# Square root and reciprocal for the first LayerNorm rows, and a new order of the first loads, turns and matmuls

## The chip, the cores and the metric

The kernel runs on one core of one Trainium2 chip. The metric is the device time of one execution in microseconds (us); less is better. The core has TensorE (matrix products, PE in the profile, with PEld for the loading of its stationary operand), VectorE (DVE), ScalarE (ACT), GpSimd (POOL) and SyncE (SP, which here only issues DMAs). 16 DMA engines move data between HBM and SBUF. PSUM has 8 buffers of 128 x 512 float32 in this kernel.

## The reference

```python
xn = layernorm(x)                       # x: 2048 rows of 512, eps 1e-5
dt, Lam = exp(log_dt), Lambda_re + 1j * Lambda_im
Lam_bar = exp(dt * Lam)
B_bar = ((Lam_bar - 1) / Lam)[:, None] * (B_re + 1j * B_im)
Bu = xn @ B_bar.T                       # 2048 x 512, complex
h[t] = Lam_bar * h[t - 1] + Bu[t]       # over 2048 steps
A = 2 * (h @ (C_re + 1j * C_im).T).real + xn * Dskip
B = (silu(xn @ w1) * (xn @ w3)) @ w2    # w1, w3: 512 x 1792, w2: 1792 x 512
out = x + A + B
```

Inputs and output are bfloat16.

## The kernel before

The 2048 rows are four blocks of 512, and a block is four groups of 128 rows. For a block the kernel normalises the rows, turns them so that the 512 columns lie on the partitions (`xnT`), multiplies by w1 and w3 in 14 tiles of 128 columns (`glu_up`, lines 372 to 397: `g_ps` and `u_ps`, then Silu and a copy on ScalarE, their product on VectorE), by the state matrices (`ssm_in`, line 402), runs the recurrence as a scan on VectorE (`ssm_tasks`, line 419), and adds the products with w2 and C into one sum (`y_out`, line 475). VectorE's work is a queue of tasks with written costs, from which `drain` takes some after each matmul tile, so the order of every engine's instructions is fixed by the program text (manual schedule); an engine runs its own in that order.

The change concerns the start, block 0 (lines 79 to 147 and 499 to 547). There:

- The loads. SP issues rows 0 to 127 and 128 to 255 (`load_rows`, lines 79 and 80), then w1 and w3 in pieces (`load_w13`, lines 111 to 116). ScalarE issues `load_prm` of Lambda_re, then rows 256 to 511 in one load, then Lambda_im and log_dt (lines 107 to 110). The three parameter vectors land in 12 rows of `prm`.
- For each group c: `stats(c)` and `aggr(c)` (VectorE: mean and variance), `rstd_act` (ScalarE, lines 167 to 170: `Ln` with the bias tensor `eps`, then `Exp` with scale -0.5; both from one table set, loaded at line 81), `normed` (VectorE, line 186), `turn` (TensorE transposes into PSUM, line 247) and `put` (a copy to `xnT`, line 251: ScalarE for groups 0 and 1, VectorE for 2 and 3).
- `keep_warm` (line 145) puts matmuls of ones on TensorE: 8 of 512 columns and 5 of 128 at the start, and 3 of 128 between the turns of groups 0 and 1.
- `ahead(w_sbs, fs, c, n)` (line 499) multiplies the rows of groups c to c+n-1 for the tiles fs of the first three glu tiles, whose PSUM buffers (`begun`) are held from the start. What is left of these tiles, rows 384 to 511, is done in `glu_up` (lines 376 to 383).
- The parameters: a TensorE transpose of `prm` (line 539) into PSUM, and `par_cols` (line 267): a ScalarE copy, an Exp for dt, small products on GpSimd. A further Exp (line 545) makes `r_col`. Then the table set with Silu is loaded (line 546).

PSUM: six buffers for the three begun tiles and two (`xt_a`, `xt_b`) for the turns. Tiles 3 and later take buffers as they come free.

The text of the start, in order (lines 508 to 547), is in the listing's end.

Of the kernel before, what the change touches and what calls it, by code (L numbers as in the profile page):

```python
# [12 lines left out]
ACT = mybir.ActivationFunctionType  # L13

FP32 = DT.float32
BF16 = DT.bfloat16
P = 128
# [3 lines left out]
def kernel(  # L21
# [24 lines left out]
    nc = tc.nc  # L46
# [9 lines left out]
    NPT = PS // P  # L56
    NFT = F // P
    assert S % TBLK == 0 and D % P == 0 and F % P == 0 and PS == NPT * P and D == 512 and NPT == 4
    LN_EPS = 1e-5
# [4 lines left out]
    const = ctx.enter_context(tc.tile_pool(name="const", bufs=1))  # L64
# [5 lines left out]
    def ps_tile(name):  # L70
        return psum.tile([P, 512], FP32, name=name, tag="ps")
# [4 lines left out]
    def load_rows(c0, c1, eng):  # L76
        eng.dma_start(out=x_blk[0][:, c0:c1, :], in_=xv[:, 0, c0:c1, :])

    load_rows(0, 1, nc.sync)
    load_rows(1, 2, nc.sync)  # L80
    nc.scalar.preload_act_table_set("natural_log_exp_and_others")
    w1_sb = const.tile([P, NDT, F], BF16, name="w1_sb")
    w3_sb = const.tile([P, NDT, F], BF16, name="w3_sb")
    w2_sb = const.tile([P, NFT, D], BF16, name="w2_sb")
# [16 lines left out]
    prm = const.tile([P, P], BF16, name="prm")  # L101
    nc.vector.memset(prm, 0.0)

    def load_prm(i, src, eng):
        eng.dma_start(out=prm[i * NPT:(i + 1) * NPT, :], in_=src.rearrange("(t p) -> t p", p=P))

    load_prm(0, A_Lambda_re, nc.scalar)
    load_rows(2, CPB, nc.scalar)
    load_prm(1, A_Lambda_im, nc.scalar)
    load_prm(2, A_log_dt, nc.scalar)  # L110
    load_w13(0, 2)
    load_w13(2, 4)
# [18 lines left out]
    eps = const.tile([P, 1], FP32, name="eps")  # L131
    nc.vector.memset(eps, LN_EPS)
    ident = const.tile([P, P], BF16, name="ident")
# [9 lines left out]
    begun = [(ps_tile("g_ps"), ps_tile("u_ps")) for _ in range(3)]  # L143

    def keep_warm(n, width=512):
        one = nc.const_aps.tensor_like(1.0, like=ident[:, 0:1])
        for _ in range(n):
            nc.tensor.matmul(out=begun[0][0][:, :width], lhsT=one.to_broadcast([P, P]), rhs=one.to_broadcast([P, width]),
                             start=True, stop=True)
# [5 lines left out]
    mv_all = const.tile([P, NBLK * CPB, 2], FP32, name="mv_all")  # L155
    rstd_all = const.tile([P, NBLK * CPB], FP32, name="rstd_all")
# [3 lines left out]
    def stats(c):  # L160
        sums[c] = work.tile([P, 6], FP32, name="stats", bufs=4)
        nc.vector.bn_stats(out=sums[c], in_=x_blk[c // CPB][:, c % CPB, :])  # L162

    def aggr(c):
        nc.vector.bn_aggr(out=mv_all[:, c, :], in_=sums.pop(c))  # L165

    def rstd_act(c0, c1):
        y = rstd_all[:, c0:c1]
        nc.scalar.activation(out=y, in_=mv_all[:, c0:c1, 1], func=ACT.Ln, bias=eps)  # L169
        nc.scalar.activation(out=y, in_=y, func=ACT.Exp, scale=-0.5)  # L170

    def rstd(c0, c1):
        y = rstd_all[:, c0:c1]
# [12 lines left out]
    def normed(c, parts=1):  # L186
        xn = work.tile([P, D], BF16, name="xn", bufs=8)
        for i in range(parts):
            ds = slice(i * D // parts, (i + 1) * D // parts)
            nc.vector.tensor_scalar(out=xn[:, ds], in0=x_blk[c // CPB][:, c % CPB, ds], scalar1=mv_all[:, c, 0:1],  # L190
                                    scalar2=rstd_all[:, c:c + 1], op0=ALU.subtract, op1=ALU.mult)
        return xn
# [51 lines left out]
    pprm = xt_a[:, NDT]  # L244
    xn0 = xns_of[0] = {}

    def turn(c, pxt, d0=0, d1=NDT):
        for dt in range(d0, d1):
            nc.tensor.transpose(out=pxt[:, dt - d0, :], in_=xn0[c][:, dt * P:(dt + 1) * P], identity=ident)  # L249

    def put(c, pxt, eng, d0=0, d1=NDT):
        dst = xnTs[0][:, d0:d1, c * P:(c + 1) * P]
        if eng is nc.scalar:
            nc.scalar.activation(out=dst, in_=pxt, func=ACT.Copy)
        else:
            nc.vector.tensor_copy(out=dst, in_=pxt)
# [3 lines left out]
    tabs = {k: const.tile([P, NPT, SB], BF16, name=f"tab_{k}") for k in ("x", "y", "c", "s")}  # L260
    col = {}

    def c4(name):
        col[name] = const.tile([P, NPT], FP32, name=f"c_{name}")
        return col[name]

    def par_cols():
        prmc = const.tile([P, 3 * NPT], FP32, name="prmc")
        nc.scalar.activation(out=prmc, in_=pprm[:, :3 * NPT], func=ACT.Copy)
        col["lre"], col["lim"], col["ldt"] = (prmc[:, i * NPT:(i + 1) * NPT] for i in range(3))  # L270
        nc.scalar.activation(out=c4("dt"), in_=col["ldt"], func=ACT.Exp)
        nc.gpsimd.tensor_tensor(out=c4("kr"), in0=col["dt"], in1=col["lre"], op=ALU.mult)
        nc.gpsimd.tensor_tensor(out=c4("ki"), in0=col["dt"], in1=col["lim"], op=ALU.mult)
        nc.gpsimd.tensor_scalar(out=c4("turn"), in0=col["ki"], scalar1=float(1.0 / (2.0 * np.pi)), scalar2=None,
                                op0=ALU.mult)
        tt = nc.gpsimd.tensor_tensor
        tt(out=c4("den"), in0=col["lre"], in1=col["lre"], op=ALU.mult)
        tt(out=c4("d2"), in0=col["lim"], in1=col["lim"], op=ALU.mult)
        tt(out=col["den"], in0=col["den"], in1=col["d2"], op=ALU.add)
# [73 lines left out]
    def drain(us):  # L353
        credit[0] = min(credit[0] + us, us + 1.5)
        while queue and credit[0] > 0:
            cost, task = queue.popleft()
            credit[0] -= cost
            task()
# [8 lines left out]
    def glu_mm(b, f, w_sb, ps, ts, dts=range(NDT)):  # L367
        for dt in dts:
            nc.tensor.matmul(out=ps[:, ts], lhsT=w_sb[:, dt, f * P:(f + 1) * P], rhs=xnTs[b][:, dt, ts],  # L369
                             start=(dt == 0), stop=(dt == NDT - 1))  # L370

    def glu_up(b, rate, begun=()):
        hg[b] = work.tile([P, NFT, TBLK], BF16, name="hgT")
        late = None
        for f in range(NFT):
            if f < len(begun):
                g_ps, u_ps = begun[f]
                ts = slice(TBLK - P, TBLK)
            else:
                g_ps, u_ps = ps_tile("g_ps"), ps_tile("u_ps")  # L380
                ts = slice(0, TBLK)
            glu_mm(b, f, w1_sb, g_ps, ts)
            glu_mm(b, f, w3_sb, u_ps, ts)
            sl16 = work.tile([P, TBLK], BF16, name="sl16", bufs=4)
            nc.scalar.activation(out=sl16, in_=g_ps, func=ACT.Silu)  # L385
            up16 = work.tile([P, TBLK], BF16, name="up16", bufs=4)
            nc.scalar.activation(out=up16, in_=u_ps, func=ACT.Copy)  # L387
            if for_act:
                for_act.popleft()()
            if late is not None:  # L390
                late()

            def late(f=f, sl16=sl16, up16=up16):
                nc.vector.tensor_tensor(out=hg[b][:, f, :], in0=sl16, in1=up16, op=ALU.mult)  # L394

            drain(rate)
        late()
# [101 lines left out]
    def ahead(w_sbs, fs, c, n=1, dts=range(NDT)):  # L499
        for f in fs:  # L500
            for w_sb in w_sbs:
                glu_mm(0, f, w_sb, begun[f][w_sb is w3_sb], slice(c * P, (c + n) * P), dts)
# [3 lines left out]
    ta, tb, t2, t3 = xt_a[:, :H], xt_b[:, :H], xt_b[:, NDT:], xt_a[:, :NDT]  # L506

    stats(0)
    aggr(0)
    rstd_act(0, 1)  # L510
    stats(1)
    aggr(1)
    rstd_act(1, 2)
    xn0[0] = normed(0, 2)
    turn(0, ta, 0, H)
    put(0, ta, nc.scalar, 0, H)
    xn0[1] = normed(1)
    turn(0, tb, H, NDT)
    put(0, tb, nc.scalar, H, NDT)
    keep_warm(3, P)  # L520
    turn(1, t1)
    put(1, t1[:, :H], nc.scalar, 0, H)
    put(1, t1[:, H:], nc.scalar, H, NDT)
    stats(2)
    aggr(2)
    rstd_act(2, 3)
    stats(3)
    ahead((w1_sb,), (0, 1), 0)
    ahead((w1_sb,), (0, 1), 1, 1, range(H))
    ahead((w1_sb,), (0, 1), 1, 1, range(H, NDT))  # L530
    xn0[2] = normed(2)
    aggr(3)
    rstd_act(3, 4)
    ahead((w3_sb,), (0, 1), 0, 2)
    turn(2, t2)
    put(2, t2, nc.vector)
    xn0[3] = normed(3)
    ahead((w1_sb,), (2,), 0, 2)
    nc.tensor.transpose(out=pprm, in_=prm, identity=ident)
    par_cols()  # L540
    ahead((w3_sb,), (2,), 0, 2)
    ahead((w1_sb, w3_sb), (0,), 2)
    turn(3, t3)
    put(3, t3, nc.vector)
    nc.scalar.activation(out=r_col, in_=col["kr"], func=ACT.Exp)
    nc.scalar.preload_act_table_set("silu_and_others")
    ahead((w1_sb, w3_sb), (1, 2), 2)

    push([(3.2, par_turns), (0.2, par_recip)])
    push([(0.0, lambda: for_act.extend(par_trig()))])  # L550
# [4 lines left out]
    push([(1.2, par_out)])  # L555
    push(ln_tasks(2))
    glu_up(0, 1.3, begun)
    assert not for_act
    ssm_in(0, 0.8)
# [3 lines left out]
    push(res_tasks(2))  # L563
    push(res_tasks(3))
    glu_up(1, 1.35)
    y_out(0, 4.0)
    ssm_in(2, 0.85)
    glu_up(2, 1.35)
    y_out(1, 4.0)
    ssm_in(3, 0.85)  # L570
# [33 lines left out]
```

## Time and profile before

| | us |
|---|---|
| median of 3 runs (lowest to highest) | 211.91 (211.91 to 212.12) |
| the profiled execution's own time | 211.86 |
| its span in the profile | 210.1 |
| TensorE busy | 205.4 |
| VectorE busy | 173.2 |
| ScalarE busy | 93.9 |
| GpSimd busy | 5.9 |
| granted TensorE clock | 0.998 |

The span is the time from the first to the last instruction of one execution on the chip, taken by the profiler. Times in the views below are us from its start. A row of the timeline has start, duration, engine, line, operation, what is written and read, the shape and the count; in square brackets stands how long the engine had been idle and what ended that. Neighbouring instructions of one line are merged into one row, so that a row's duration covers all of them. The duration of a matmul is modelled to the end of its pipeline; the distance from one start to the next is what TensorE spends on it.

Busy time by stage, from the view by windows (each engine's us and instruction count):

| window, us | PE | DVE | ACT |
|---|---|---|---|
| 0.00 to 4.88 | 4.01 (14) | 2.06 (9) | 2.04 (4) |
| 4.88 to 7.02 | 2.05 (27) | 1.98 (5) | 1.79 (8) |
| 7.02 to 11.95 | 4.93 (76) | 3.18 (10) | 3.40 (9) |
| 11.95 to 69.10 | 56.83 (262) | 53.83 (132) | 43.08 (76) |
| 69.10 to 210.10 | 137.55 (650) | 112.20 (193) | 43.62 (73) |

### The profile page before, as it was taken

The page shows a single profiled execution, that of the slowest core. Times are in us where ns is not written, and L with a number is a line of the kernel's source. Part 1 is how long each engine was busy: PE and PEld are TensorE (multiplying, and loading weights), DVE is VectorE, ACT ScalarE, POOL GpSimd, SP SyncE. Part 2 cuts the span into 40 slices and gives each one's busy share as a digit, 9 for nine tenths or more (in the row PEclk, how much of TensorE's full clock was granted, in tenths as well). Part 3 has the DMA queues.
Part 4 walks back from the last instruction along what each step waited for, and adds up shares of the span by engine and source line. Part 5 has one row for each costly group of instructions (what it writes and reads, how often), then busy time and mean ns, then how long its engine had stood idle before and what let it go on. Part 6 is the DMA issues. An engine that isn't in the chain of part 4 may idle for free.

```text
span 210.1 us, 2867 instructions
## 1 busy us (share of the span) xinstructions
PE 205.4 (98%) x1021; PEld 97.7 (47%) x1039; DVE 173.2 (82%) x345; ACT 93.9 (45%) x167; POOL 5.9 (3%) x27
## 2 busy tenths in 40 slices
PE   8999999999999999999999999999999999999994
PEld 3864444444444444444444444444444444444453
DVE  4699989979999999999999999999999999121111
ACT  4699867666666200066666500036666620000000
POOL 2100410000000000000000000000000000000000
PEclk9999999999999999999999999999999999999999
DMA  6999798965000000000004100100000000000110
GB/s 172 299 353 199 106 189 179 329 133 106 19 3 0 0 25 25 28 27 0 0 0 78 27 16 9 50 28 0 2 0 0 0 3 25 27 25 25 44 34 25
DMA packets 27094, 13.69 MB, mean 65 GB/s; under 512 B 15944, under 2 KB 27080, under 8 KB 27080
## 3 DMA queue, kind: packets, MB, share of 16 engines
q1 hardware_dynamic: 26784, 13.24, 26.8%
q10 hardware_dynamic: 296, 0.27, 0.4%
q8 instruction: 8, 0.13, 0.3%
q14 instruction: 6, 0.05, 0.1%
HBM read 7.74 MB, written 2.10 MB: 47 GB/s over the span
## 4 chain that ended last, share of the span: by engine, by line
PE 95%; DVE 1%; ACT 1%; DMA 1%; issue 1%; ACTq 0%
PE u_ps L369 23%; PE y_ps L485 23%; PE g_ps L369 22%; PE y_ps L490 13%; PE bu_ps L408 13%; DMA x_blk<-in_A_x_dram 1%; ACT up L387 1%; DVE stats L162 1%; PE xt_ps L249 0%; DVE xn L190 0%; PE g_ps L249 0%; DVE mv_all L165 0%; ACT rstd_all L169 0%; DVE o L495 0%; ACT rstd_all L170 0%
## 5 line engine op out<-in xcount | busy, mean ns | idle before, releaser
L369 PEld LDWEIGHTS <-w_sb 128*128 128x128 bf16 x504 | 46.6, 98 | 50.1
L369 PE MATMUL u_ps<-xnT,w_sb 128*128 128x512 bf16 (+2 forms) x247 | 58.3, 358 | 0.3
L369 PE MATMUL g_ps<-xnT,w_sb 128*128 128x512 bf16 (+2 forms) x249 | 57.6, 352 | 0.2
L485 PE MATMUL y_ps<-w_sb,hgT 128*128 128x512 bf16 (+2 forms) x233 | 50.7, 366 | 0.2
L387 ACT ACTIVATE up<-u_ps 128x512 bf16<-128x512 f32 x56 | 33.8, 603 | 15.2 <-PE u_ps L369 14.9
L410 ACT ACTIVATE u<-bu_ps 128x512 bf16<-128x512 f32 x32 | 19.1, 598 | 46.3 <-PE bu_ps L408 46.3
L385 ACT ACTIVATE sl<-g_ps 128x512 bf16<-128x512 f32 x56 | 33.7, 602 | 9.8 <-PE g_ps L369 8.2
L442 DVE TENSOR_TENSOR_SCAN ab<-r_col,h,ab 128x256 bf16<-128x256 f32 x56 | 37.7, 732 | 0.2
L485 PEld LDWEIGHTS <-hgT 128*128 128x128 bf16 x238 | 22.8, 98 | 25.9
L495 DVE TENSOR_TENSOR o<-y_ps,x_blk 128x512 bf16<-128x512 f32 (+2 forms) x17 | 11.1, 654 | 24.3 <-PE y_ps L490 24.3
L490 PE MATMUL y_ps<-ct,h 128*128 128x512 bf16 (+2 forms) x134 | 30.2, 366 | 0.1
L408 PE MATMUL bu_ps<-xnT,bt 128*128 128x512 bf16 x125 | 27.8, 379 | 0.2
L394 DVE TENSOR_TENSOR hgT<-sl,up 128x512 bf16<-128x512 bf16 x56 | 23.0, 414 | 2.2 <-ACT up L387 2.2
L490 PEld LDWEIGHTS <-h 128*128 128x128 bf16 x136 | 13.0, 98 | 14.7
L408 PEld LDWEIGHTS <-bt 128*128 128x128 bf16 x128 | 12.5, 98 | 15.1
L162 DVE BATCH_NORM_STATS2 stats<-x_blk 128x6 f32<-128x512 bf16 x16 | 10.6, 674 | 2.0 <-DMA x_blk<-in_A_x_dram 2.0
L451 DVE TENSOR_TENSOR ab<-ab,tab_s 128x2048 bf16<-128x2048 bf16 x8 | 9.8, 1224 | 0.2
L447 DVE TENSOR_TENSOR ab<-ab,tab_c 128x2048 bf16<-128x2048 bf16 x8 | 9.8, 1222 | 0.1
L427 DVE TENSOR_TENSOR ab<-u,tab_y 128x2048 bf16<-128x2048 bf16 x8 | 9.8, 1219 | 0.0
L424 DVE TENSOR_TENSOR ab<-u,tab_x 128x2048 bf16<-128x2048 bf16 x8 | 9.8, 1219 | 0.0
L199 DVE TENSOR_TENSOR x_blk<-xd,x_blk 128x512 bf16<-128x512 bf16 x16 | 6.8, 426 | 0.5
L198 DVE TENSOR_TENSOR xd<-xn,dskip_row 128x512 bf16<-128x512 bf16 x16 | 6.7, 418 | 0.0
(74 smaller groups left out, 80.1 us busy)
## 6 DMA issues: line engine op xcount, KB each, us to landing
w_sb<-in_B_w_dram SPq DMA_DIRECT2D x4, 512.0 KB, 7.7
out_dram<-o SPq DMA_DIRECT2D x15, 128.0 KB, 1.7
w_sb<-in_B_w_dram SPq DMA_DIRECT2D x1, 1792.0 KB, 9.1
w_sb<-in_B_w_dram SPq DMA_DIRECT2D x6, 256.0 KB, 4.8
x_blk<-in_A_x_dram SPq DMA_DIRECT2D x3, 512.0 KB, 5.9
x_blk<-in_A_x_dram SPq DMA_DIRECT2D x2, 128.0 KB, 2.1
x_blk<-in_A_x_dram ACTq DMA_DIRECT2D x1, 256.0 KB, 3.6
xnT<-xn SPq DMA_TRANSPOSE x12, 2.5
```

The costliest lines, as they stand in the source:

```text
L162: nc.vector.bn_stats(out=sums[c], in_=x_blk[c // CPB][:, c % CPB, :])
L369: nc.tensor.matmul(out=ps[:, ts], lhsT=w_sb[:, dt, f * P:(f + 1) * P], rhs=xnTs[b][:, dt, ts], start=(dt == 0), stop=(dt == NDT - 1))
L385: nc.scalar.activation(out=sl16, in_=g_ps, func=ACT.Silu)
L387: nc.scalar.activation(out=up16, in_=u_ps, func=ACT.Copy)
L394: nc.vector.tensor_tensor(out=hg[b][:, f, :], in0=sl16, in1=up16, op=ALU.mult)
L408: nc.tensor.matmul(out=u_ps, lhsT=bt[ri][:, dt, pt * P:(pt + 1) * P], rhs=xnTs[b][:, dt, :], start=(dt == 0), stop=(dt == NDT - 1))
L410: nc.scalar.activation(out=u16[:, :, pt, ri, :], in_=u_ps.rearrange("p (s t) -> p s t", s=NSB), func=ACT.Copy)
L424: nc.vector.tensor_tensor(out=ab[0][:, :, 0:2, :], in0=u16, in1=tab_b("x"), op=ALU.mult)
L442: nc.vector.tensor_tensor_scan(out=a[:, pt, 2 * ri + 1, :], data0=r_b, data1=a[:, pt, 2 * ri, :], initial=init, op0=ALU.mult, op1=ALU.add)
L485: nc.tensor.matmul(out=y_ps[:, ds], lhsT=hg[b][:, f, cl * P:(cl + 1) * P], rhs=w2_sb[:, f, ds], start=(f == 0), stop=False)
L490: nc.tensor.matmul(out=y_ps[:, ds], lhsT=h_tiles[i][:, pt, ri, h_ts], rhs=ct[ri][:, pt, ds], start=False, stop=(pt == NPT - 1 and ri == 1))
L495: nc.vector.tensor_tensor(out=o16[:, ds], in0=y_ps[:, ds], in1=x_blk[b][:, cl, ds], op=ALU.add)
```

## The change

ScalarE now makes the square root of variance plus 1e-5, with the constant in the instruction in place of the `eps` tensor, and VectorE makes its reciprocal (`rstd_inv`), which stands in VectorE's order where the diff puts it. The first table set is the one with Sqrt, and after group 3's Sqrt the set with Exp is loaded; Silu's set follows as before. On ScalarE's DMA queue, Lambda_im goes ahead of rows 256 to 511. The transpose of the parameters and ScalarE's copy of them become `par_turn`, ahead of group 3's aggregate. The turns of groups 2 and 3 stand together, behind all `ahead` pieces of rows 0 to 255 except tile 2 of w3, and tiles 1 and 2 take rows 256 to 511 in one piece of 256 columns, so that `glu_up` has matmuls of rows 384 to 511 for tile 0 alone. One of the three `keep_warm` matmuls goes.

```diff
-    nc.scalar.preload_act_table_set("natural_log_exp_and_others")
+    nc.scalar.preload_act_table_set("sqrt_and_others")
...
     load_prm(0, A_Lambda_re, nc.scalar)
+    load_prm(1, A_Lambda_im, nc.scalar)
     load_rows(2, CPB, nc.scalar)
-    load_prm(1, A_Lambda_im, nc.scalar)
     load_prm(2, A_log_dt, nc.scalar)
...
     def rstd_act(c0, c1):
         y = rstd_all[:, c0:c1]
-        nc.scalar.activation(out=y, in_=mv_all[:, c0:c1, 1], func=ACT.Ln, bias=eps)
-        nc.scalar.activation(out=y, in_=y, func=ACT.Exp, scale=-0.5)
+        nc.scalar.activation(out=y, in_=mv_all[:, c0:c1, 1], func=ACT.Sqrt, bias=LN_EPS)
+
+    def rstd_inv(c):
+        y = rstd_all[:, c:c + 1]
+        nc.vector.reciprocal(out=y, in_=y)
...
+    prmc = const.tile([P, 3 * NPT], FP32, name="prmc")
...
+    def par_turn():
+        nc.tensor.transpose(out=pprm, in_=prm, identity=ident)
+        nc.scalar.activation(out=prmc, in_=pprm[:, :3 * NPT], func=ACT.Copy)
+
     def par_cols():
-        prmc = const.tile([P, 3 * NPT], FP32, name="prmc")
-        nc.scalar.activation(out=prmc, in_=pprm[:, :3 * NPT], func=ACT.Copy)
...
-            glu_mm(b, f, w1_sb, g_ps, ts)
-            glu_mm(b, f, w3_sb, u_ps, ts)
+            if f == 0 or f >= len(begun):
+                glu_mm(b, f, w1_sb, g_ps, ts)
+                glu_mm(b, f, w3_sb, u_ps, ts)
...
     rstd_act(0, 1)
     stats(1)
+    rstd_inv(0)
     aggr(1)
     rstd_act(1, 2)
     xn0[0] = normed(0, 2)
     turn(0, ta, 0, H)
     put(0, ta, nc.scalar, 0, H)
+    rstd_inv(1)
     xn0[1] = normed(1)
     turn(0, tb, H, NDT)
     put(0, tb, nc.scalar, H, NDT)
-    keep_warm(3, P)
+    keep_warm(2, P)
     turn(1, t1)
...
     rstd_act(2, 3)
     stats(3)
+    rstd_inv(2)
     ahead((w1_sb,), (0, 1), 0)
     ahead((w1_sb,), (0, 1), 1, 1, range(H))
     ahead((w1_sb,), (0, 1), 1, 1, range(H, NDT))
-    xn0[2] = normed(2)
+    par_turn()
     aggr(3)
     rstd_act(3, 4)
+    nc.scalar.preload_act_table_set("exp_and_others")
+    xn0[2] = normed(2)
+    rstd_inv(3)
+    xn0[3] = normed(3)
     ahead((w3_sb,), (0, 1), 0, 2)
+    ahead((w1_sb,), (2,), 0, 2)
     turn(2, t2)
     put(2, t2, nc.vector)
-    xn0[3] = normed(3)
-    ahead((w1_sb,), (2,), 0, 2)
-    nc.tensor.transpose(out=pprm, in_=prm, identity=ident)
+    turn(3, t3)
+    put(3, t3, nc.vector)
     par_cols()
     ahead((w3_sb,), (2,), 0, 2)
     ahead((w1_sb, w3_sb), (0,), 2)
-    turn(3, t3)
-    put(3, t3, nc.vector)
     nc.scalar.activation(out=r_col, in_=col["kr"], func=ACT.Exp)
     nc.scalar.preload_act_table_set("silu_and_others")
-    ahead((w1_sb, w3_sb), (1, 2), 2)
+    ahead((w1_sb, w3_sb), (1, 2), 2, 2)
```

## The prediction

> **What bounds the kernel now.** I read the page's busy times first, then the chain that ended last, then the timeline of the first 13 us, instruction by instruction where merged rows hide starts.
>
> ```profile
> PE 205.4 (98%) x1021; PEld 97.7 (47%) x1039; DVE 173.2 (82%) x345; ACT 93.9 (45%) x167; POOL 5.9 (3%) x27
> ...
> PE 95%; DVE 1%; ACT 1%; DMA 1%; issue 1%; ACTq 0%
> ```
>
> TensorE is busy 98% of the span and makes 95% of the chain. Only a few us at the start belong to others. The change edits only those, so the question is when TensorE begins to run without a gap, and whether it gets a new one. In the timeline:
>
> ```profile
> 2.88 0.69 DVE L162 BATCH_NORM_STATS2 stats<-x_blk 128x6 f32<-128x512 bf16 x1 [1.95 <-DMA x_blk<-in_A_x_dram]
> ...
> 3.83 0.29 ACT L169 ACTIVATE rstd_all<-mv_all,eps 128x1 f32<-128x1 f32 x1 [1.83 <-DVE mv_all L165]
> 4.16 0.20 ACT L170 ACTIVATE rstd_all<-rstd_all 128x1 f32<-128x1 f32 x1
> 4.41 0.18 DVE L165 BATCH_NORM_AGGREGATE mv_all<-stats 128x2 f32<-128x6 f32 x1
> 4.50 1.10 DVE L190 TENSOR_SCALAR xn<-x_blk,mv_all,rstd_all 128x256 bf16<-128x256 bf16 x3
> 4.62 0.29 ACT L169 ACTIVATE rstd_all<-mv_all,eps 128x1 f32<-128x1 f32 x1 [0.27 <-DVE mv_all L165]
> ...
> 4.95 0.20 ACT L170 ACTIVATE rstd_all<-rstd_all 128x1 f32<-128x1 f32 x1
> ...
> 5.65 0.23 PEld L249 LDWEIGHTS <-xn 128*128 128x128 bf16 x4 [0.24 <-DVE xn L190]
> ...
> 6.09 0.66 ACT L254 ACTIVATE xnT<-g_ps 128x256 bf16<-128x256 bf16 x2 [0.23 <-PE g_ps L249]
> ...
> 7.02 1.04 PE L369 MATMUL u_ps<-xnT,w_sb 128*128 128x256 bf16 x8
> ```
>
> The reader is to see one chain: rows 0 land (2.86), VectorE's statistics, ScalarE's Ln and Exp for rows 128 to 255, VectorE's normalisation (5.185 to 5.601, the third of the x3), TensorE's turn (5.658), ScalarE's copies (6.092 to 6.750), TensorE's matmuls. From 7.022 on, every start to start distance is the matmul's own (0.056 us for 128 columns, 0.109 for 256, 0.216 for 512); a double one every 10.79 us is a missing record. So time moves only by what moves 7.022, by the sum of columns behind it, or by a new gap.
>
> **Sqrt and reciprocal for Ln and Exp.** No row shows Sqrt. Nearest: Exp without a bias tensor 0.202 us, a 12-column Copy 0.181, Ln with its bias tensor 0.295. I take 0.20, ends 0.18 and 0.295. RECIPROCAL on 128x4 took 0.172, other 128x4 VectorE operations 0.161 to 0.170. I take 0.17.
> Rows 0: Sqrt starts at 3.83 like Ln and ends at 4.03. The reciprocal stands behind the second statistics, whose 0.66 us free VectorE at about 4.285 for independent work, while the aggregate that needs their result starts at 4.406. In that hole of 0.12 us the reciprocal needs some 0.09 (14.04, and the next operation 14.13). Cost nothing; without the hole 0.09.
> Rows 128 to 255: Sqrt at 4.623 to 4.82 (4.92 at the upper end). But the reciprocal is queued on VectorE behind the two halves of the first normalisation, at 4.505 and 4.735. These free it after 0.23 to 0.26 us: 4.965 to 4.993. Add 0.17 and the 0.03 that a dependent operation waits: the normalisation starts at 5.165 to 5.195, where before it started at 5.185, 0.034 after Exp ended. So 0.33 us leave ScalarE's chain, and VectorE's queue is late next. Gain nothing (between 0.02 and -0.01). The warm-up matmul removed was inside TensorE's wait that ended at 5.658: nothing.
>
> **Order behind 7.022.** Before, TensorE did 8 matmuls of 256, 4 turns, 4 of 256, the parameter turn, 4 of 256, 8 of 128, 4 turns and 40 of 128: 0.874+0.224+0.437+0.056+0.437+0.447+0.224+2.235 = 4.93 us, until 11.95. After: parameter turn 7.08, first 8 until 7.95, 4 until 8.39, both turns until 8.84, 4 until 9.27, tile 0's 8 of 128 until 9.72, 16 of 256 (1.747) until 11.47, tile 0's last 8 until 11.91. That is 32 matmuls of 128 (1.788) turned into 16 of 256 (1.747): gain 0.04.
> New waits: rows 256 to 383 are copied by VectorE behind both turns' starts. Turn 2 ends at 8.56+0.219 = 8.775, the copy (start 0.038 later, 0.425 long) at 9.24, TensorE has it 0.05 later at 9.29; due 9.27. Cost 0.02. The second copy ends at 9.58, due 9.72. Nothing.
>
> ```profile
> 8.55 0.22 PE L539 MATMUL xt_ps<-ident,prm 128*128 128x128 bf16 x1
> ...
> 8.81 0.18 ACT L269 ACTIVATE prmc<-xt_ps 128x12 f32<-128x12 bf16 x1 [0.54 <-PE xt_ps L539]
> ...
> 9.77 1.28 ACT L546 ACT_TABLE_LOAD   x1
> ...
> 11.06 0.60 ACT L385 ACTIVATE sl<-g_ps 128x512 bf16<-128x512 f32 x1
> ```
>
> The parameter turn moves from 8.555 to 7.02, and ScalarE's copy of it (7.28) now stands before the Sqrt of rows 384 to 511, which therefore starts at 7.38, not at 7.26 when its aggregate is done. Then: end 7.58, reciprocal 7.61, normalisation 7.81 to 8.23, TensorE has it at 8.28; due 8.61. Covered by 0.33.
> The extra table load: ScalarE 7.60 to 8.88, Exp 8.90, GpSimd's product, Exp 9.43, the next load 9.65 to 10.93. Silu of tile 0 waits for TensorE anyway, which now closes tile 0's sum at 11.69 (data 11.87), against 11.06 before. Silu is thus 0.8 later; cover 0.94. TensorE needs a PSUM buffer from it first at tile 4: tile 3's first matmul waits, by its semaphore, for TensorE alone, tile 4's (13.68) for ScalarE. Silu and copy of tile 0 end at 12.47 and 13.0, due 13.64 and 14.5. VectorE behind it has more room: the first state tile is written at 56.1 and read at 71.95, the next at 71.85 and 81.45. Cost nothing.
>
> The Trainium skill, "ScalarE: Activation LUTs", section "Table sets: the hidden batching unit", speaks against this change: ln and exp share one set and one load, while exp and sqrt lie in different sets, some 2.7 us for each switch. The trace does not agree on the size: its load took 1.28 us, with Silu 0.01 behind it. With the page's figure for both loads the estimate would be 2.8 us more on ScalarE.
>
> **The loads.** Rows 256 to 511 are issued at 1.531 now; a parameter issue ahead (0.373 us, with gaps up to 0.475) makes it about 1.93. They landed at 5.11 by the semaphore. Later by 0.40 alone is 5.51; as the weights take most of the DMA engines from 4.5 on, up to twice that, 5.9. Their statistics start at 5.52, behind the normalisation, so a wait of 0 to 0.4 comes. The ends: it is free until 5.95 (0.12 from the parameter copy, 0.33 at turn 3), above that one for one. The third parameter load still follows them on ScalarE's queue. It landed at 6.67, needed now at 7.02. The bytes ahead of it are the same, so I take 6.7; the upper end is 6.67+0.8 = 7.47, a stall of 0.45. On SP's queue the first weights landed at 5.70 for a use at 5.89, and could come 0.3 later when the rows share their packets. TensorE is idle from 6.34 to 6.53, so 0.18 of this is free. The next w1 tiles landed at 7.50, due 7.95. Cost nothing, range 0 to 0.15.
>
> **Sum.** -0.04 + 0.02 + 0 = about -0.03 on the profiled execution's 211.86 (span 210.1 and 1.76 around it): 211.83. The median of the runs shown is 0.05 above it, so 211.88. About 0.2% (0.42 us) is what a measurement of this kernel can tell from no change.
>
> **The rivals.**
> 1. Loads late (slower). Behind the delayed rows the third parameter load lands after 7.02, and TensorE stops there, with ScalarE's Sqrt behind it. For: it landed only 0.35 before that. Against: nothing new is ahead of it in its queue. It decides from a landing at 7.02 on, one for one. At the upper end, 7.47, it costs 0.45; the same late rows then push the first weights too (0.15). Together 211.88 + 0.60 = 212.5. Chance 0.17, of which 0.13 for a size above 0.45, since the two waits have one cause and come together, and 0.04 for less.
> 2. ScalarE's chain was the true bound. If VectorE takes the reciprocal as soon as Sqrt ends (4.85), the normalisation starts at 5.05, 0.13 earlier: 211.88 - 0.13 = 211.75. Against: queue order. Chance 0.08. For more than 0.42 the whole idle time of TensorE from 5.43 to 6.80 would have to shrink by half (211.4): chance 0.06, since no step does that.
> 3. Table loads cost more than their row. If each of the two kept ScalarE for twice its row, 2.56 in place of 1.28, Silu of tile 0 would start at 10.93+2.56 = 13.49 and end at 14.09; TensorE would have its buffer at 14.14, due 13.64: 0.5 lost, 212.4. Chance 0.02, since Silu stood 0.01 behind the load at 11.06. By the page named above (2.7 us a switch) it would be some 0.3 more; the trace does not bear that out.
> 4. The moves don't do what they say: the same columns at the same pace, and a hidden reciprocal. That is my forecast, 211.88, chance 0.67.
>
> **How the numbers follow.** Within 0.2%: the forecast (0.67), rival 2's smaller form (0.08) and the milder part of rival 1 (0.04): 0.79. Slower: 0.13 from rival 1 and 0.02 from rival 3: 0.15. Faster: 0.06. The range takes in rival 2's smaller form with the spread of runs, and rival 1 to its upper end: 211.6 to 212.5.
>
> **What the new profile would show.** The second reciprocal starts near 4.98 and the normalisation of rows 128 to 255 near 5.19 (step right), or at 5.05 (rival 2). The statistics of rows 256 to 383 wait for a DMA until 5.5 to 5.9. TensorE's parameter turn starts near 7.03 with no idle time; idle time there that ends with a DMA is rival 1. TensorE's first 512-column matmul starts near 11.92. Three table loads of 1.28. Wrong I am if a gap stands between 7.02 and 13.7, or if the chain's head ends before 6.9.

## The result and the profile after

| | before | after |
|---|---|---|
| median, us (22 runs each) | 211.91 | 212.25 |
| lowest to highest | 211.78 to 212.25 | 211.87 to 214.1 |
| profiled execution's own time / span | 211.86 / 210.1 | 212.49 / 210.7 |

The ratio is 1.0017 with a 95% interval of 1.0009 to 1.0025: slower by 0.34 us (0.19 to 0.53 by that interval), where 0.03 less was forecast. The profiled execution is 0.24 above the median of its kernel, so its sum below is larger than 0.34, and its terms are those of one slower execution.

The chain that ended last, on the page of the kernel after, by engine and by line:

```profile
PE 95%; DMA 3%; DVE 0%; issue 0%
PE u_ps L376 23%; PE y_ps L493 23%; PE g_ps L376 23%; PE y_ps L498 13%; PE bu_ps L416 13%; DMA prm<-in_A_log_dt_dram 2%; DMA x_blk<-in_A_x_dram 1%; PE xt_ps L252 0%; DVE o L503 0%; PE xt_ps L273 0%
```

VectorE's and ScalarE's steps at the start have left the chain. In their place stands a load of 1 KB, the third parameter vector, with 2% of the span. Its piece in the chain, asked in order of time (start, us, what):

```profile
2.86 4.76 DMA prm<-in_A_log_dt_dram
```

The timeline shows what waited (start, duration, engine; in brackets the idle time and what ended it):

```profile
4.97 0.16 DVE L173 RECIPROCAL rstd_all<-rstd_all 128x1 f32<-128x1 f32 x1
5.16 0.41 DVE L193 TENSOR_SCALAR xn<-x_blk,mv_all,rstd_all 128x512 bf16<-128x512 bf16 x1
...
6.21 0.69 DVE L162 BATCH_NORM_STATS2 stats<-x_blk 128x6 f32<-128x512 bf16 x1 [0.63 <-DMA x_blk<-in_A_x_dram]
...
6.51 0.90 PEld L376 LDWEIGHTS <-w_sb 128*128 128x128 bf16 x16 [0.55 <-DMA w_sb<-in_B_w_dram]
...
7.66 0.10 PEld L273 LDWEIGHTS <-prm 128*128 128x128 bf16 x1 [0.25 <-DMA prm<-in_A_log_dt_dram]
...
10.26 1.28 ACT L559 ACT_TABLE_LOAD   x1
...
12.56 0.60 ACT L393 ACTIVATE sl<-g_ps 128x512 bf16<-128x512 f32 x1 [1.01 <-PE g_ps L376]
```

The reciprocal and the normalisation stand where they were forecast (4.97; 5.162, against 5.185 before). Three waits end with a DMA: the statistics of rows 256 to 383, the first w1, the last parameters. Silu waits for TensorE, not for a table load.

Landings by the semaphores, before and after: rows 256 to 511 at 5.11 and 6.18, first w1 at 5.70 and 6.47, third parameter vector at 6.67 and 7.62. Yet the rows are issued only 0.27 later (1.531 and 1.800), and w1 at the same 1.638 in both. The order of the two issues has changed. ACTq and SPq are the issuing queues of ScalarE and SP; in the kernel before:

```profile
1.53 0.45 ACTq L77 DMA_DIRECT2D x_blk<-in_A_x_dram  x1
...
1.64 0.43 SPq L90 DMA_DIRECT2D w_sb<-in_B_w_dram  x1
```

and after:

```profile
1.64 0.43 SPq L90 DMA_DIRECT2D w_sb<-in_B_w_dram  x1
...
1.80 0.40 ACTq L77 DMA_DIRECT2D x_blk<-in_A_x_dram  x1
```

TensorE's time from start to start: its first weighted matmul moves from 5.892 to 6.518. The waits of 0.19 and 0.05 for ScalarE's copies, which stood behind it, are gone, so 0.40 is left when these 16 matmuls end. Add 0.245 for the parameters, 0.02 for the VectorE copy (9.818 to 9.946), take off 0.04 for the wider matmuls: 0.62. The first matmul of 512 columns starts at 12.583 against 11.951, 0.63 later, and the spans differ by 0.6.

### The profile page after: what moved, and what is told of

Same layout as the page of the kernel before. It is cut to its first block, busy times and chain, and to the rows that moved or that the text cites. A ratio compares the mean times of both kernels' runs of the same rounds, so it can differ in the third digit from the quotient of the medians.

```text
span 210.7 us, 2848 instructions
## 1 busy us (share of the span) xinstructions
PE 206.8 (98%) x1022; PEld 97.6 (46%) x1022; DVE 173.9 (83%) x349; ACT 93.5 (44%) x164; POOL 6.0 (3%) x27
## 4 chain that ended last, share of the span: by engine, by line
PE 95%; DMA 3%; DVE 0%; issue 0%
PE u_ps L376 23%; PE y_ps L493 23%; PE g_ps L376 23%; PE y_ps L498 13%; PE bu_ps L416 13%; DMA prm<-in_A_log_dt_dram 2%; DMA x_blk<-in_A_x_dram 1%; PE xt_ps L252 0%; DVE o L503 0%; PE xt_ps L273 0%
## 5 line engine op out<-in xcount | busy, mean ns | idle before, releaser
L395 ACT ACTIVATE up<-u_ps 128x512 bf16<-128x512 f32 x56 | 34.3, 612 | 15.5 <-PE u_ps L376 15.5
L393 ACT ACTIVATE sl<-g_ps 128x512 bf16<-128x512 f32 x56 | 34.2, 610 | 10.2 <-PE g_ps L376 10.0
```

## The experiments

Theory 1: the order of ScalarE's loads costs it all, because the rows now come behind the first w1 load in the order of issue; the early parameter turn and TensorE's first weights wait for what lands late. Theory 2: the new order of turns, square roots and matmuls costs it. Each result stands beside the kernel before on the same chip. Landings and waits are those of each run's one profiled execution.

| run | median, us | before | ratio, 95% interval |
|---|---|---|---|
| e1_loads_back | 211.83 | 211.87 | 0.9996 (0.9987 to 1.0005) |
| e2_loads_only | 212.11 | 211.87 | 1.0011 (1.0002 to 1.0019) |
| e3_turn_late | 212.86 | 211.87 | 1.0045 (1.0033 to 1.0058) |
| e4_w1_behind_rows | 211.86 | 211.87 | 1.0001 (0.9992 to 1.0010) |
| e5_turn_mid | 212.04 | 211.90 | 1.0004 (0.9995 to 1.0013) |
| e6_warm3 | 212.09 | 211.90 | 1.0008 (0.9999 to 1.0017) |
| e7_rows_on_sp | 211.97 | 211.90 | 1.0003 (0.9994 to 1.0011) |
| e8_rows_last | 214.15 (one run) | 211.90 | |
| e9_rows_first | 212.38 | 211.89 | 1.0027 (1.0016 to 1.0039) |
| e10_back_and_mid | 211.87 | 211.89 | 0.9998 (0.9990 to 1.0007) |

**e1_loads_back**, from the kernel after:

```diff
-    load_prm(1, A_Lambda_im, nc.scalar)
     load_rows(2, CPB, nc.scalar)
+    load_prm(1, A_Lambda_im, nc.scalar)
```

> The changed kernel with the old order of ScalarE's loads (rows 256 to 511 ahead of Lambda_im), all else as changed. Theory 1, the loads' order costs it all: the rows are issued near 1.53 again, ahead of the first w1 load at 1.64, land near 5.1, w1 near 5.7, the last parameters near 6.7; TensorE's wait for w1 and for the parameters go, and the time is that of the kernel before or 0.04 less: 211.85 to 211.95. Theory 2, the new order of turns, Sqrt and matmuls costs it: stays at 212.2 or more.

Rows landed at 4.86, w1 at 5.71, the parameters at 6.65; no wait for a DMA is left on TensorE. 211.83: theory 1 holds, and theory 2 falls. Everything else in the change together, with the loads in the old order, is worth 0.04 less, not told apart from nothing.

**e2_loads_only**: the opposite edit, in the kernel before.

> The kernel before with the new order of ScalarE's loads alone. Theory 1: rows land near 6.2, w1 near 6.5, TensorE's first weighted matmul at 6.5 in place of 5.9; the parameter turn at 8.5 or later does not wait, so the cost is that of the weights and perhaps of group 2: 212.1 to 212.3. Theory 2: 211.9, as before.

212.11. Rows landed at 5.98, w1 at 6.14; the first weighted matmul started at 6.182. The parameter turn, at 8.65, did not wait; the matmuls behind it waited 0.16 for a later w3 piece. So the loads' order alone, without the early parameter turn, costs 0.24 (0.04 to 0.40 by its interval). In this profile little of that is the first w1: it came 0.29 later, but the waits for ScalarE's copies behind it shrank, and the matmuls of 256 columns started 0.07 later (7.09 for 7.02).

**e3_turn_late**, from the kernel after:

```diff
-    par_turn()
     aggr(3)
...
     put(3, t3, nc.vector)
+    par_turn()
     par_cols()
```

> The changed kernel with the parameter turn and its copy moved back behind the turns of groups 2 and 3, the loads as changed. Theory 1: the wait for the last parameter load (0.25 in the profile of the changed kernel) goes, the wait for w1 (0.55) stays: 0.2 to 0.25 less than the changed kernel, 212.0. If the parameter wait only hides another (group 2's rows landing at 6.2): 212.2.

212.86, outside both forecasts: the edit brought a wait of its own. Its timeline:

```profile
8.83 0.91 DVE L259 COPY xnT<-xt_ps 128x512 bf16<-128x512 bf16 x2
...
9.79 0.22 PE L273 MATMUL xt_ps<-ident,prm 128*128 128x128 bf16 x1 [0.52 <-DVE xnT L259]
```

The parameter turn writes the PSUM buffer in which group 3 was turned, in other columns, and the program makes it wait until VectorE has copied group 3 out. TensorE lost 0.68 there, more than the parameters' wait that it was to remove. The profile also has a wait of 0.25 between the turns of groups 2 and 3, for the normalisation of group 3, whose rows came late. So this run tells nothing of the parameters; e5 asks that again.

**e4_w1_behind_rows**, from the kernel after (SP issues it behind rows 128 to 255, ahead of w1):

```diff
-    load_prm(2, A_log_dt, nc.scalar)
+    load_prm(2, A_log_dt, nc.sync)
     load_w13(0, 2)
```

> The changed kernel with the load of log_dt moved from ScalarE's queue to SP's, just ahead of the first w1 load: the rows' load is still issued near 1.80, but w1 now near 1.95 or later, behind it. Theory 1a, what counts is which of the two is issued first: the rows' first packets come near 3.0 (4.0 in the changed kernel) and they land near 5.4; w1 lands near 6.0; time 211.85 to 212.0. Theory 1b, what counts is the 0.27 us of delay of the rows alone, whatever else is issued: they land at 6.0 to 6.2 as in the changed kernel, time 212.0 to 212.2 (the parameter wait goes in either case).

The rows were issued at 1.811, as late as in the kernel after, and landed at 4.98 instead of 6.18. w1 was issued 0.4 later than there, at 2.036, and landed at 5.65 instead of 6.47. A plain delay (1b) can't do that: what counts is which of the two is issued first. 211.86, as the kernel before. The edit also takes log_dt from behind the rows (it landed at 3.40), but in e1, where log_dt stands behind them, the rows were as early. (In the profiled execution, 212.25, the next w1 piece landed at 8.19 and cost 0.39.) What the DMA engines did shows in the stretch from 3 to 4 us (the last two columns are their share and GB/s), first the kernel before:

```profile
3.00:4.00 1.00, 1.00 (x4) 0.30 (x2) 0.96 (x3) 0.17 (x1) 0.00 (x0) 1.00 0.70 214
```

the kernel after:

```profile
3.00:4.00 1.00, 1.00 (x4) 0.30 (x2) 0.97 (x3) 0.19 (x1) 0.00 (x0) 1.00 0.33 49
```

and this experiment:

```profile
3.00:4.00 1.00, 1.00 (x4) 0.30 (x2) 0.96 (x3) 0.20 (x1) 0.00 (x0) 1.00 0.80 206
```

After the change the DMA engines move 0.17 MB less in this 1 us (49 GB/s against 214), with both loads already issued. At the 324 GB/s of the next us (kernel after, 4 to 5) that is 0.5 us of transfers that are made up later, by all that is queued.

The 12 profiles divide by the order of the two issues. In the five with w1 0.16 to 0.18 ahead of the rows (the kernel after, e2, e3, e5, e6) 49 to 136 GB/s move from 3 to 4 us, the rows land at 5.98 to 6.21, w1 at 5.96 to 6.47 and the parameters at 6.80 to 7.62. In the other seven, with the rows ahead of w1 or, in e8, 1.2 us behind it, 206 to 314 GB/s move there. Three of these have the kernel before's order (before, e1, e10): rows at 4.86 to 5.11, w1 at 5.68 to 5.71, parameters at 6.46 to 6.67. The packets in the traces, which queue and size tell apart (1,024 bytes for the rows, 512 for w1), show the same: before, the rows' first packet starts at 2.74 and w1's at 3.48; after, w1's at 2.76 and the rows' at 4.08, and only 132 of w1's packets start before 4.0, against 479 in e8 below.

**e5_turn_mid**, from the kernel after:

```diff
-    par_turn()
     aggr(3)
     rstd_act(3, 4)
-    nc.scalar.preload_act_table_set("exp_and_others")
...
     ahead((w3_sb,), (0, 1), 0, 2)
+    par_turn()
+    nc.scalar.preload_act_table_set("exp_and_others")
```

> The changed kernel with the parameter turn behind the first eight matmuls of 256 columns (and the load of the Exp set behind ScalarE's copy of it), the loads as changed. Theory 1, TensorE waits for two landings, w1's and the last parameters': w1's wait stays (first weighted matmul at 6.1 to 6.5), the parameter turn comes near 8.3, where its data are there, so its wait of 0.25 goes; 212.0 to 212.1. Theory 2, only w1's wait counts and TensorE would wait for group 2 or 3 in the parameters' place: 212.2 to 212.3.

212.04: 0.14 above the kernel before beside it, and 0.21 under the median of the kernel after, but the intervals of the two ratios overlap. The parameters landed at 6.80 and TensorE did not wait for them; w1 landed at 6.14 and it waited for that. So the parameters' wait goes with the edit, as theory 1 says; that it is worth 0.2 is likely and not shown by the times. In this profile TensorE's slow pace at the start (see e6) costs more than w1's wait: six of the first weighted matmuls, from 6.18 on, took 0.08 to 0.11 us each instead of 0.056.

**e6_warm3**: `keep_warm(3, P)` in the kernel after.

> The changed kernel with three warm-up matmuls again. If the loads cost it all, 212.25 as the changed kernel, with the same three late landings (rows 6.0 to 6.3, w1 6.0 to 6.5, parameters 7.1 to 7.7). If the removed matmul lets the clock come up later (in the changed kernel's profile matmuls of 128 columns still took 0.107 us at 5.9), 211.9 to 212.0, and the clock is up by 4.5.

212.09, with the late landings: rows 6.20, w1 5.96, parameters 7.11. It lies between what the two theories gave, and its interval touches those of both the kernel before and the one after. The clock gives no reason to suspect the removed matmul: matmuls of 128 columns take 0.107 us at first and 0.056 later, and the first at the fast pace stood between 3.77 and 6.79 in the eight profiles with two warm-up matmuls, between 3.98 and 5.87 in the four with three. These ranges overlap, and four are few. Whether it costs a tenth of a us stays open.

The waits of this profile differ from those of the kernel after: the parameters cost TensorE 0.18 and the late normalisation of group 3 cost 0.12, while w1 landed 0.5 earlier than there and cost nothing (the 16 matmuls that wait for it ended at 6.98, against 7.02 in the kernel before). Which of the late landings TensorE pays for changes from one profile to the next, so the split of the median's 0.34 into single waits stays open.

**e7_rows_on_sp**, from the kernel after:

```diff
-    load_rows(2, CPB, nc.scalar)
+    load_rows(2, CPB, nc.sync)
```

> The changed kernel with the load of rows 256 to 511 on SP's queue, just ahead of the first w1 load. Theory 1a (which is issued first): rows land at 5.0 to 5.4, w1 at 5.6 to 6.0 although it is issued 0.4 later, 211.8 to 211.95. Theory 1b (a plain delay of what is issued later): w1 lands at 6.1 or later and TensorE waits for it, 212.0 to 212.2.

211.97. w1, issued at 2.111, 0.47 later than in the kernel after, landed at 6.15, 0.3 earlier than there; the rows at 5.37. 15 of w1's 16 parts were there by 5.47, one was late. The landing misses the range given and the time agrees with 1a: inconclusive by itself, in line with e4. It also prices w1 alone, as no other load was late for TensorE here: the first weighted matmul came 0.30 later than in the kernel before, but what follows these 16 matmuls started at 7.09, 0.07 later.

**e8_rows_last**, from the kernel before: the rows behind all three parameter loads.

> The kernel before with rows 256 to 511 behind all three parameter loads (issued near 2.9 to 3.1). What holds w1 up: if it is that the rows' packets come between its own, w1 lands near 5.3 to 5.6, earlier than in the kernel before (5.70); if it is that the first load behind rows 128 to 255 starts slowly, whichever it is, w1 lands at 6.0 or later with the rows out of its way. Rows land near 7.0, so the time is 212.3 or more in either case.

With the rows issued at 2.81, w1 landed at 4.97, earlier than in any other run, and 227 GB/s moved from 3 to 4 us. So w1 alone does not start slowly; it is slow when the rows are issued 0.16 behind it. The rows themselves landed at 8.18, not 7.0, and TensorE stood for 2.25 us before group 2's turn:

```profile
8.20 0.69 DVE L162 BATCH_NORM_STATS2 stats<-x_blk 128x6 f32<-128x512 bf16 x1 [2.67 <-DMA x_blk<-in_A_x_dram]
```

**e9_rows_first**, from the kernel after: the rows ahead of all three parameter loads.

> The changed kernel with rows 256 to 511 first on ScalarE's queue, ahead of all three parameter loads. If being issued ahead of w1 is what counts, rows land at 5.1 or earlier, w1 at 5.4 to 5.7, 211.8 to 211.9, no better than with the rows second, since TensorE's start hangs on rows 0 to 255. If the rows now take the place of rows 0 to 255, those land later than 2.86 and 3.32 and the whole head moves by that: 212.0 to 212.5.

212.38: the second case. Issued at 0.745, between rows 0 to 127 (0.72) and rows 128 to 255 (1.181), they landed at 3.82, but rows 128 to 255 then landed at 4.16 instead of 3.32:

```profile
4.19 0.69 DVE L162 BATCH_NORM_STATS2 stats<-x_blk 128x6 f32<-128x512 bf16 x1 [0.19 <-DMA x_blk<-in_A_x_dram]
```

In the kernel before, these statistics started at 3.71. Being issued ahead again let a load land ahead, here to the harm of rows 128 to 255, and rows 0 to 127, though issued first, came later too (3.06 for 2.86). w1 landed at 6.16, later than the 5.4 to 5.7 of the first case; why is open, and it cost nothing, since the whole head was 0.5 later.

**e10_back_and_mid**: e1's and e5's edits together.

> The changed kernel with the old order of the loads and the parameter turn behind the first eight matmuls of 256 columns: both causes undone. If they are the whole cost, 211.83 as with the loads alone undone (no wait for the parameters was left there), against 212.25 for the changed kernel and 211.9 for the one before.

211.87 against 211.89: with both edits undone nothing of the cost is left, as with e1 alone. No version tried is shown to be faster than the kernel before: e1's interval holds 1.

## Why the prediction was wrong

The time, 212.25, lies inside the range of 211.6 to 212.5, and the difference inside the 0.2% (0.42 us) that the prediction took for the least to be told from no change. Neither is to its credit: 22 runs told 0.34 from nothing, and the upper end of the range came from rival 1, which the prediction argued against. Its own sign of being wrong came, too: a gap between 7.02 and 13.7, here 0.245 before the parameter turn at 7.67.

- **What bounds the kernel** was right: the time moved by TensorE's gaps in the first 13 us and nothing else.
- **Sqrt and reciprocal** came as worked out: 0.194 to 0.203 and 0.145 to 0.165 us for 0.20 and 0.17; the normalisation at 5.162 for 5.165 to 5.195 (the first statistics started 0.02 earlier). It brought nothing, since VectorE's queue was next, as said.
- **Order behind 7.022**: the columns saved 0.04 and the copy cost 0.02, as said, and the table loads were hidden. e1 is 0.04 under the kernel before, as forecast (0.03), though this size lies inside its interval.
- **The loads** is the step that failed. It took the rows "later by 0.40", up to twice that, and the parameters at "6.7", because "the bytes ahead of it are the same". The issue moved even less than assumed (0.27). But I looked at ScalarE's queue alone, and weighed SP's w1 load only by the packets that it would share. That load is issued at 1.638: the rows stood 0.107 ahead of it before and stand 0.16 behind it now. The runs showed in the step's place that passing this point costs the rows 1.07 us, w1 0.77 and the parameters 0.95 in the profile (w1 0.26 to 0.43 and the parameters 0.13 to 0.44 in the other four with this order), while the DMA engines move 49 GB/s for 1 us instead of 214. The 0.5 us of transfers lost by that would account for about half of the rows' lateness; the rest fits their lost place, as they landed 0.59 ahead of w1 before and beside it after. This adding up is an estimate, and why the engines move so little stays open.
- **"Cost nothing, range 0 to 0.15"** for w1 was therefore 0.40 in the profile, and the parameter wait, put at 0 with an upper end of 0.45, was 0.245. The sizes are those of this execution: at a w1 landing of 6.14 to 6.15 (e2, e7) w1 alone cost 0.07, within the range given, and in e2 another 0.16 came from a later w3 piece, which the prediction had not looked at. Rival 1 named the waiting instructions and the point from which they wait, but not why the loads would be that late; its argument against, "nothing new is ahead of it in its queue", was true of the queue and beside the point.
- The lateness of rows 256 to 511 was free until 5.95 by the prediction. They landed at 6.18, and the turns had the room only because TensorE was itself late; where it was less late, group 3's turn waited (0.12 in e6, 0.25 in e3).
- **Rival 3**, dearer table loads, fell: three loads of 1.28 us, and Silu waited 1.01 for TensorE. The rule of the Trainium skill ("ScalarE: Activation LUTs", section "Table sets: the hidden batching unit", 2.7 us for each switch) is not what the trace shows.

## What to carry to other kernels

When a load is moved on one queue, write out the issue times of all loads on all queues and see which ones it passes: here 0.27 us of delay made a load land about 1 us later, because one load of another queue lay in between. Before an instruction at the head of an in-order engine is given an earlier place, look up when the last of its inputs lands; a 1 KB load that nobody had waited for became a piece of 4.76 us in the chain. And undo the parts one by one: with the edit that looked like housekeeping (the order of two loads) undone, nothing was left of the cost, and the arithmetic that the change is named for held none. Read the waits of more than one profile before a cost is split among them.

## What the runs showed of the hardware

- The order of issue across the two hardware queues, at a distance of 0.1 to 0.2 us, decided which 256 KB load's packets started first (rows at 2.74 and w1 at 3.48 before, w1 at 2.76 and rows at 4.08 after). With w1 ahead, the DMA engines were busy for 0.33 of the us from 3 to 4, against 0.70 with the rows ahead, and the load issued first did not land first: w1 landed at 6.47, the rows at 6.18. With the rows 1.2 us behind w1 (e8) the share was 0.85. Why, the records don't show; that stays open. The Trainium skill, "DMA: Bandwidth & Descriptors", section "Issuing engines are not separate DMA queues", says that DMAs of all issuing engines interleave on the same 16 DMA engines and that issuing from several saves only issue time. The trace of the kernel after agrees that the loads interleave: from 4.08 to 5.5 us packets of both start in every half us. But more than issue time hung on the order of issue: the rows landed 1.07 us later for an issue 0.27 later.
- A load of 1 KB took 4.76 us from issue to landing behind a 256 KB load on its queue (3.79 in the kernel before), where the first parameter vector, first on its queue at 0.945, had landed 1.94 later, at 2.89 (kernel before).
- The moment from which matmuls of 128 columns run at 0.056 us lay anywhere between 3.77 and 6.79 us in the 12 profiles, while the clock column read 1.00 all along. In e5's profile the slow pace cost TensorE 0.27 us in the first weighted matmuls. No edit can be seen to move it.
